# A new start of the written order of a recurrence and a two-layer product: three leading products of zeros fewer, the summing matrices finished in four steps

## The chip, the cores and the metric

One Trainium2 chip, one core. The metric is the device time of one execution in microseconds. The kernel before takes 308.44 us (median of 3 runs, 307.92 to 308.74).

## The reference

First a chunked linear recurrence (4 batches, 8 heads, 768 positions, head width 32, state width 16), then a two-layer product over its 3072 rows of 256:

```python
log_a = np.log(np.clip(a, 1e-06, 1.0))
for c in range(nc):                                  # chunks of 32 positions
    cum = np.cumsum(la, axis=-1)
    L = np.exp(cum[:, :, :, None] - cum[:, :, None, :]) * causal
    M = np.einsum('bhin,bhjn->bhij', Cc, Bc) * L
    y[:, :, sl] = (np.einsum('bhij,bhjd->bhid', M, xc)
                   + np.einsum('bhin,bhnd->bhid', Cc, state) * np.exp(cum)[:, :, :, None])
    Bx = np.einsum('bhjn,bhjd->bhjnd', Bc, xc) * np.exp(cum[:, :, -1:] - cum)[:, :, :, None, None]
    state = np.exp(np.sum(la, axis=-1))[:, :, None, None] * state + np.sum(Bx, axis=2)
...
h = x @ w_in                                         # 256 to 2048
g = np.maximum(h, 0.0) + np.log1p(np.exp(-np.abs(h)))
out = g @ w_out                                      # 2048 to 256
```

## The kernel before

The 768 positions of a batch are six units of 128, 24 units in all, and units go in pairs that share a load tile (`un`). The two products run beside the recurrence as its units become ready; after the recurrence they run alone until the end. Each float32 operand of a large product is split into a rounded part and a rest (`xh`, `xl`, `wih`, `wil`), and three products of the parts are added.

All of it is driven by one written table, `ORDER` (L50), a text of words. The loop at the end of the kernel takes them one by one; a word's name is looked up in `acts` and its numbers are the arguments. `InOrder` and `keep_in_program_order` keep the instructions of every engine, SP's loads too, in the order in which the words emit them. A function that is `staged` does one piece at each of its words, up to its next `yield`. So the table is the order of each engine's queue. `BANKS` holds, digit by digit, which PSUM bank each next request gets.

The words that matter here, with the names that the profile shows:

- `warm3`: products of zeros on TensorE (`some`, 128x512), as many as the number says. They compute nothing that is used.
- `la`, `lr`: loads of the decay factors by column and by row; `loga`, `logr`: a clip on VectorE, then a log on ScalarE; `gb` spreads the log of la (`logs`).
- `kc`: `sums_on_chip` (L201). VectorE fills a tile, GpSimd cuts triangles out of it, and four steps of VectorE make the four summing matrices of 32, 64, 96 and 128 columns.
- `ft`, `fr`: the factors of a batch. Five products of `la` with blocks of `kc` (two passes each), then ScalarE's exponentials `fc` and `ft`; `by_head` on VectorE and a product give `fr`. The growth factors `gg` of the first four units come from `gq` (kc,logs on TensorE).
- `growth`: a scan and an Exp in place of `lr`; `gd`: its store to DRAM in four DMAs; `gg4`: a load from there, the growth factors of the pair 4 and 5. Later pairs have theirs the same way.
- `B` (`bp`), `Q` (C times growth, in place), `C` (`cc`), `A` (`parts_c`, on ScalarE) prepare a pair; `D` makes the masks `rm` on GpSimd; `S` is the score product, `M` weighs it on VectorE (`m`), `U` updates the state, `T` spreads it (`tb`), `R` and `I` make a unit's result, `G` and `X` round it and take the rest (`xh`, `xl`).
- `v`, `un`, `hc`: loads of units. A load tile of `un` can be loaded again when the products that read it are done: the first load behind `w1` goes into the tile of units 4 and 5, whose last reader is `I5`.
- `w4` (and w0, w2, w6): the load of two feature tiles of w_in; `W4`, in pieces, splits it: `ends` on ScalarE, `w` on VectorE, `wih` on ScalarE, `wil` on VectorE. `F`, `H` are the first product over 512 and 256 rows, `P` the parts of its activation (`e`, `gh`, `gl`), `Z` the second product. `F0.4` is the first over 512 rows to read w4's columns. ScalarE loads another activation table ahead of the first `e`.

The three lines that make a staged function:

```python
            if (f, args) not in stages:
                stages[f, args] = f(*args)
            next(stages[f, args], None)
```

Of the kernel before, what the change touches and what calls it, by code (L numbers as in the profile page):

```python
# [999 lines left out]
```

## Time and profile before

| | us |
|---|---|
| median of the runs | 308.44 |
| the profiled execution, its own time | 309.62 |
| its span, first to last instruction | 307.9 |
| TensorE busy (matmuls) | 302.2 |
| VectorE busy | 252.4 |
| ScalarE busy | 176.4 |
| GpSimd busy | 41.1 |

The profiled execution took 309.62 us, of which 307.9 lie between its first and its last instruction. Busy times are sums over the span; they don't tell which engine is waited for at a given moment. Times of the rows further down count from the start of the span.

### The profile page before, as it was taken

The numbers are of one execution on the slowest core, as the hardware profiler recorded it, in microseconds if no ns is written. First come the engines' busy times: TensorE is split into PE (matmuls) and PEld (weight loads), VectorE is DVE, ScalarE is ACT, GpSimd is POOL, SyncE is SP. The second block draws the span as 40 slices with busy tenths as digits, with TensorE's granted clock in tenths as the row PEclk, the third lists the DMA queues.
The fourth block names the chain that finished last, engine by engine and source line by source line (L and its number), as shares of the span: only waits on it lengthen the run. The fifth ranks groups of instructions, "written<-read, shape, count | busy, mean of one in ns | idle before, by whom it ended". The sixth has DMA issues, their size and how long they took to land.

```text
span 307.9 us, 5844 instructions
## 1 busy us (share of the span) xinstructions
PE 302.2 (98%) x2275; PEld 242.9 (79%) x2275; DVE 252.4 (82%) x501; ACT 176.4 (57%) x318; POOL 41.1 (13%) x62
## 2 busy tenths in 40 slices
PE   8999999999999999999999999999999999999995
PEld 5778678778878777788888888888888888888884
DVE  5998898697787868999889898998978858776873
ACT  5568576755755525363666477355566466364662
POOL 2723211440303262100000000000000000000000
PEclk9999999999999999999999999999999999999999
DMA  6992984353203001000010000000012000000003
GB/s 191 311 390 81 351 309 138 131 194 119 73 2 105 0 29 42 2 3 0 33 37 0 0 2 0 0 1 2 1 47 89 2 0 0 1 2 0 0 2 136
DMA packets 10684, 21.77 MB, mean 71 GB/s; under 512 B 1184, under 2 KB 4640, under 8 KB 10656
## 3 DMA queue, kind: packets, MB, share of 16 engines
q1 hardware_dynamic: 10656, 21.40, 20.1%
q8 instruction: 18, 0.29, 0.4%
q14 instruction: 10, 0.08, 0.1%
HBM read 17.85 MB, written 3.54 MB: 69 GB/s over the span
## 4 chain that ended last, share of the span: by engine, by line
PE 91%; DVE 4%; DMA 2%; POOL 1%; issue 1%; ACT 0%; SPq 0%; POOLq 0%
PE sums_at L176 91%; DMA un<-in_un 2%; DVE gl L171 1%; POOL rm L176 1%; DVE wol L171 1%; DVE xl L171 0%; DVE m L171 0%; DVE again L171 0%; DVE state L171 0%; ACT xh L176 0%; SPq L185 0%; DVE cc L171 0%; DVE w L171 0%; DVE bp L171 0%; ACT gh L176 0%
## 5 line engine op out<-in xcount | busy, mean ns | idle before, releaser
L176 PE MATMUL sums_at<-gh,woh 128*128 128x512 f32 (+1 forms) x194 | 76.0, 392 | 0.0
L176 PE MATMUL sums_at<-gl,woh 128*128 128x512 f32 (+1 forms) x194 | 75.4, 389 | 0.0
L176 PE MATMUL sums_at<-gh,wol 128*128 128x512 f32 (+1 forms) x194 | 75.1, 387 | 0.0
L171 DVE TENSOR_TENSOR gl<-e,gh 128x512 fp32r<-128x512 f32 x96 | 63.9, 684 | 12.6 <-ACT gh L176 12.6
L176 ACT CAST gh<-e 128x512 fp32r<-128x512 f32 x96 | 58.7, 620 | 12.5 <-PE sums_at L176 10.8
L176 POOL TENSOR_SCALAR_AFFINE_SELECT rm<-fc 128x512 f32<-128x512 f32 (+1 forms) x52 | 39.8, 789 | 83.8 <-DVE tb L171 19.6
L176 ACT ACTIVATE e<-e 128x512 f32<-128x512 f32 x48 | 30.0, 630 | 23.9 <-DVE e L171 23.8
L176 PEld LDWEIGHTS sums_at<-gh,woh 128*128 128x128 f32 x194 | 36.4, 188 | 8.5 <-issue 0.6
L176 PEld LDWEIGHTS sums_at<-gl,woh 128*128 128x128 f32 x194 | 36.4, 188 | 8.0 <-DVE gl L171 0.8
L176 PEld LDWEIGHTS sums_at<-gh,wol 128*128 128x128 f32 x194 | 36.4, 188 | 7.4
L176 ACT ACTIVATE e<-sums_at 128x512 f32<-128x512 f32 x48 | 28.3, 593 | 23.0 <-PE sums_at L176 18.0
L176 PE MATMUL sums_at<-xh,wih 128*128 128x512 f32 (+1 forms) x104 | 39.8, 383 | 0.0
L176 PE MATMUL sums_at<-xl,wih 128*128 128x512 f32 (+1 forms) x104 | 38.9, 374 | 0.0
L176 PE MATMUL sums_at<-xh,wil 128*128 128x512 f32 (+1 forms) x104 | 38.8, 373 | 0.0
L171 DVE TENSOR_TENSOR e<-sums_at,u 128x512 f32<-128x512 f32 x48 | 32.4, 686 | 6.9 <-PE sums_at L176 6.3
L171 DVE TENSOR_TENSOR m<-sums_at,rm 128x512 f32<-128x512 f32 x48 | 31.4, 685 | 7.3 <-POOL rm L176 4.9
L171 DVE TENSOR_TENSOR u<-sums_at,u 128x512 f32<-128x512 f32 x32 | 22.0, 688 | 4.5 <-PE sums_at L176 3.6
L176 PE MATMUL sums_at<-sxih,sw 128*128 128x512 f32 x64 | 23.8, 390 | 0.0
L176 PEld LDWEIGHTS sums_at<-xh,wih 128*128 128x128 f32 x104 | 19.5, 188 | 4.3
L176 PEld LDWEIGHTS sums_at<-xh,wil 128*128 128x128 f32 x104 | 19.6, 188 | 3.6
L176 PEld LDWEIGHTS sums_at<-xl,wih 128*128 128x128 f32 x104 | 19.6, 188 | 3.2
L176 ACT CAST sw<-sums_w 128x512 fp32r<-128x512 f32 x16 | 9.9, 620 | 13.8 <-DVE sums_w L171 13.7
(109 smaller groups left out, 405.5 us busy)
## 6 DMA issues: line engine op xcount, KB each, us to landing
un<-in_un SPq DMA_DIRECT2D x20, 320.0 KB, 4.6
wraw<-in_w_in SPq DMA_DIRECT2D x8, 511.8 KB, 5.1
wraw<-in_w_out SPq DMA_DIRECT2D x8, 511.8 KB, 6.2
out_t<-o SPq DMA_DIRECT2D x11, 256.0 KB, 2.0
gg<-gd SPq DMA_DIRECT2D x10, 128.0 KB, 5.1
head_in<-in_un SPq DMA_DIRECT2D x4, 192.0 KB, 2.9
head_in<-in_un SPq DMA_DIRECT2D x4, 128.0 KB, 3.1
gd<-lr SPq DMA_DIRECT2D x4, 96.0 KB, 4.5
```

Of the source, the lines that this page charges most:

```text
L171: last_of_v[0] = f(*a, **k)
L176: return lambda *a, **k: tc.keep_in_program_order(f(*a, **k))
```

## The change

The first 195 words of `ORDER` become 199, and the first 45 digits of `BANKS` go with them. The 1080 words from `gg14 X5 F0.5` on are the old ones. As a multiset the new words are the old ones but for two: `warm6` is now `warm3` (so the first real product of TensorE has six products of zeros ahead of it instead of nine), and `kc` stands five times instead of once, since `sums_on_chip` yields ahead of each of its four last steps and is staged now. No other instruction is added or removed; the rest of the change moves instructions within the queues.

```diff
-kc la loga loga gb ends warm1 warm1 warm1 warm6 ft0 lr logr logr growth growth ft0 kb ft0 ft0 fr0 fr2 fr2 D1 fr0
-gq0 gq0 un1 fr0 fr0 un0 hc0 hc1 B0 Q0 C0 hc2 D0 ft0 gq2 warm1 gq2 D0 D0 un3 U0 U1 U0 U1 A0 S0 ft2 ft2 M0 D0 M0
...
-w2 W2 W2 ft2 gd warm1 warm1 T3 G1 X1 S2 w0 W0 un5 W0 M2 W2 M2 fr2 warm1 warm1 fr2 un4 w4 B4 W0 W0 R2 D4 W2 R3 D4
-I3 U3 G3 X3 I2 G2 X2 U4 U3 gg4 Q4 W4 H1 W4 un6 un7 U4 gg6 B6 Q6 D5 A4 D5 w6 W4 H3 T5 F0.1 H0 F0.0 P0.0 S4 F0.3
...
+warm3 la warm1 kc warm1 kc loga kc warm1 un1 loga hc0 lr un0 kb kc ends kc ft0 hc2 hc1 gb logr logr ft0 hc3 ft0
+gq0 growth ft0 gq0 fr0 B0 fr0 gq2 ft0 Q0 fr2 fr0 gq2 D1 fr0 D0 A0 D0 D1 warm1 U0 U1 D1 D0 Q2 U0 fr2 S0 D0 ft2
+fr2 D1 ft2 C2 fr2 un2 un3 growth ft2 M0 C0 M0 ft2 U1 w0 T1 B2 w2 S1 warm1 D3 M1 un4 U2 warm1 A2 ft2 W0 warm1 M1
...
+U3 I2 G3 G2 un7 gd v8 D4 W2 un5 gg4 w4 X2 X3 v10 un6 W2 Q4 A4 W2 v9 w6 gg6 H1 H0 F0.1 D4 D5 P0.1 S4 F0.0 H3 C4
...
         for c in range(NC):
             n = SUB * (c + 1)
+            yield
             V.tensor_scalar(kc[:, c * P : c * P + n], later[:, :n], part[:, c : c + 1], 1.0, op0=ALU.add, op1=ALU.subtract)
...
-        "kc": sums_on_chip,
+        "kc": staged(sums_on_chip),
```

VectorE's queue at the start of the program, before (kc are the summing matrices, la the clip, ends the clearing of two tiles of the weight split):

```order
L171 TENSOR_SCALAR kc_74<-kc_74 128x32
L171 TENSOR_SCALAR kc_74<-kc_74 128x64
L171 TENSOR_SCALAR kc_74<-kc_74 128x96
L171 TENSOR_SCALAR kc_74<-kc_74 128x128
L171 TENSOR_SCALAR la_71<-la_71 128x192
L171 MEMSET ends0_83 128x512
L171 MEMSET ends1_84 128x512
L171 TENSOR_SCALAR lr_72<-lr_72 128x192
```

and in the changed kernel:

```order
L171 TENSOR_SCALAR kc_74<-kc_74 128x32
L171 TENSOR_SCALAR la_71<-la_71 128x192
L171 TENSOR_SCALAR kc_74<-kc_74 128x64
L171 TENSOR_SCALAR kc_74<-kc_74 128x96
L171 MEMSET ends0_83 128x512
L171 MEMSET ends1_84 128x512
L171 TENSOR_SCALAR kc_74<-kc_74 128x128
L171 TENSOR_SCALAR lr_72<-lr_72 128x192
L171 SCALAR_TENSOR_TENSOR cum_73<-keep_82,lr_72 128x192
```

The clip of la comes forward by three places; the fourth step of kc goes behind both clearings.

VectorE's queue further on, before, from the first factors to the first weighing m0 (`head_in<-head_in,gg` is C times growth of the first pair with gg0 and of the second with gg2):

```order
L171 TENSOR_TENSOR by_head2_137<-sums_at_69,kb_75 96x60
L171 TENSOR_TENSOR by_head0_141<-sums_at_69,kb_75 96x60
L171 TENSOR_TENSOR bp0_154<-head_in_80,ft0_130 128x256
L171 TENSOR_TENSOR head_in_80<-head_in_80,gg0_143 128x2x128
L171 TENSOR_TENSOR cc0_157<-head_in_80,fr0_149 128x128
L171 COPY state0_179<-sums_at_69 128x64
L171 SCALAR_TENSOR_TENSOR state1_181<-state0_179,fr0_149,sums_at_69 128x64
L171 TENSOR_TENSOR m0_200<-sums_at_69,rm0_160 128x512 x2
L171 TENSOR_TENSOR tb2_220<-state1_181,kb_75 128x64
```

and in the changed kernel:

```order
L171 TENSOR_TENSOR bp0_142<-head_in_80,ft0_130 128x256
L171 TENSOR_TENSOR by_head0_144<-sums_at_69,kb_75 96x60
L171 TENSOR_TENSOR head_in_80<-head_in_80,gg0_134 128x2x128
L171 TENSOR_TENSOR head_in_80<-head_in_80,gg2_146 128x2x128
L171 COPY state0_175<-sums_at_69 128x64
L171 TENSOR_TENSOR by_head2_177<-sums_at_69,kb_75 96x60
L171 TENSOR_TENSOR cc2_198<-head_in_80,fr0_156 128x256
L171 TENSOR_TENSOR m0_206<-sums_at_69,rm0_158 128x512
L171 TENSOR_TENSOR cc0_208<-head_in_80,fr0_156 128x128
L171 TENSOR_TENSOR m0_206<-sums_at_69,rm0_158 128x512
L171 SCALAR_TENSOR_TENSOR state1_212<-state0_175,fr0_156,sums_at_69 128x64
```

bp0 comes ahead of by_head; the second pair's C times growth and its cc, which stood behind m0 and m1, now stand ahead of m0's two halves or between; the first update of the state (state1) moves behind them.

ScalarE's queue around its second table load, before (ends1_84 with wraw4 is the first piece of w4's split, wih_76 with w4 the third):

```order
L176 CAST ends1_84<-wraw4_323 128x512
L176 ACTIVATE parts_c_85<-un2_310,kb_75 128x256
L176 CAST wih_76<-w4_374 128x2x256
L176 ACT_TABLE_LOAD
L176 ACTIVATE e0_0_426<-sums_at_69 128x512
L176 ACTIVATE e0_1_442<-sums_at_69 128x512
```

and in the changed kernel:

```order
L176 CAST wih_76<-w2_296 128x2x256
L176 ACTIVATE parts_c_85<-un2_235,kb_75 128x256
L176 ACT_TABLE_LOAD
L176 ACTIVATE e0_1_403<-sums_at_69 128x512
L176 CAST ends1_84<-wraw4_367 128x512
L176 CAST wih_76<-w4_431 128x2x256
L176 ACTIVATE e0_0_452<-sums_at_69 128x512
```

Both pieces of w4's split move from ahead of the table load to behind it and behind the first e.

SP's queue from the first load of w_in on, before (gd the stores of lr, gg4 the first load from there):

```order
L185 DMA wraw2_282<-in_w_in 128x2047
L185 DMA gd_81<-lr_72 32x4x192 x4
L185 DMA wraw0_306<-in_w_in 128x2047
L185 DMA un2_310<-in_un 128x640 x2
L185 DMA wraw4_323<-in_w_in 128x2047
L185 DMA gg4_371<-gd_81 128x1x256
```

and in the changed kernel:

```order
L185 DMA wraw0_214<-in_w_in 128x2047
L185 DMA wraw2_220<-in_w_in 128x2047
L185 DMA un2_235<-in_un 128x640
L185 DMA un3_353<-in_un 128x640
L185 DMA gd_81<-lr_72 32x4x192 x4
L185 DMA un4_359<-in_un 128x640
L185 DMA un2_235<-in_un 128x640
L185 DMA gg4_365<-gd_81 128x1x256
L185 DMA wraw4_367<-in_w_in 128x2047
```

The four stores stand behind both w and two units instead of behind one w, and the load of w4 moves from ahead of gg4 to behind it. ScalarE's Exp of lr, which the stores wait for, moves from the fifth place of its queue behind the factors fr2 of the second batch, the fifteenth.

## Rows read from the trace of the kernel before

**Rows 1.** The page's fourth part: shares of the chain that ended last, by engine.
```profile
PE 91%; DVE 4%; DMA 2%; POOL 1%; issue 1%; ACT 0%; SPq 0%; POOLq 0%
```

**Rows 2.** The chain in order of time, whole span: start us, us, what.
```profile
18.27 0.68 issue
18.95 9.38 PE sums_at L176 x131
...
30.15 5.30 DMA un<-in_un
...
35.95 57.49 PE sums_at L176 x597
```

**Rows 3.** Timeline of SP's issues: start us, us, then engine, line, operation, count.
```profile
6.68 2.58 SPq L185 DMA_DIRECT2D gd<-lr  x4
...
12.65 0.58 SPq L185 DMA_DIRECT2D gg<-gd  x1
...
29.10 0.33 SPq L185 DMA_DIRECT2D un<-in_un  x1
```

**Rows 4.** Timeline of TensorE, 25 to 29.2 (columns as before, with partitions, size, type).
```profile
25.39 0.39 PE L176 MATMUL sums_at<-xh,wil 128*128 128x512 f32 x1
...
26.39 0.50 PE L176 MATMUL sums_at<-un 16*128 16x128 f32 x8
...
28.33 0.66 PE L176 MATMUL sums_at<-m,un 128*32 128x128 f32 x16
```

**Rows 5.** Two stretches: us, busy us of each engine, clock, DMA share, GB/s.
```profile
9.85:18.30 8.45, 8.41 (x154) 6.13 (x153) 8.45 (x20) 4.80 (x13) 3.97 (x7) 1.00 0.97 347
23.50:29.00 5.50, 5.50 (x125) 4.44 (x128) 4.47 (x11) 4.01 (x9) 2.48 (x4) 1.00 0.17 64
```

**Rows 6.** Timeline of TensorE, the start; the brackets tell idle time and its releaser.
```profile
0.98 4.02 PE L176 MATMUL sums_at<-some 128*32 128x512 bf16 x9 [0.98 <-POOL some L176]
...
4.93 1.11 PE L176 MATMUL sums_at<-la,kc 128*128 128x96 f32 x4
```

**Rows 7.** Timeline of VectorE, 0 to 23.
```profile
3.68 1.02 DVE L171 MEMSET ends<- 128x512 int32 x2
...
7.01 0.34 DVE L171 TENSOR_TENSOR by_head<-sums_at,kb 96x60 f32<-96x60 f32 x2 [0.81 <-PE sums_at L176]
7.33 0.71 DVE L171 TENSOR_TENSOR bp<-head_in,ft 128x256 f32<-128x256 f32 x1
...
9.85 1.29 DVE L171 TENSOR_TENSOR m<-sums_at,rm 128x512 f32<-128x512 f32 x2 [0.26 <-PE sums_at L176]
...
11.18 0.42 DVE L171 TENSOR_TENSOR bp<-head_in,ft 128x256 f32<-128x256 f32 x1
...
16.91 1.28 DVE L171 TENSOR_TENSOR m<-sums_at,rm 128x512 f32<-128x512 f32 x2
...
20.60 0.52 DVE L171 TENSOR_TENSOR un<-un,gg 128x256 f32<-128x256 f32 x1
...
22.64 0.68 DVE L171 TENSOR_TENSOR wil<-w,wih 128x512 fp32r<-128x512 f32 x1
```

**Rows 8.** Timeline of ScalarE, 6 to 25.
```profile
6.74 0.52 ACT L176 ACTIVATE fc<-sums_at 128x192 f32<-128x192 f32 x1
...
11.03 0.52 ACT L176 ACTIVATE fc<-sums_at 128x192 f32<-128x192 f32 x1 [1.88 <-PE sums_at L176]
...
19.93 0.78 ACT L176 CAST ends<-wraw 128x512 f16<-128x512 bf16 x1
...
22.39 1.28 ACT L176 ACT_TABLE_LOAD   x1
23.68 1.08 ACT L176 ACTIVATE e<-sums_at 128x512 f32<-128x512 f32 x2
```

**Rows 9.** Timeline of GpSimd (POOL), 7 to 24.
```profile
7.33 3.63 POOL L176 TENSOR_SCALAR_AFFINE_SELECT rm<-fc 128x256 f32<-128x256 f32 x8 [4.68 <-ACT ft L176]
```

**Rows 10.** DMA issues from 12.6 to 13.2: KB, us from issue to landing.
```profile
gg<-gd SPq DMA_DIRECT2D x1, 128.0 KB, 6.3
```

More of the change, by code (lines that the diff above doesn't have):

```diff
@@ new lines @@
+fr2 D1 ft2 C2 fr2 un2 un3 growth ft2 M0 C0 M0 ft2 U1 w0 T1 B2 w2 S1 warm1 D3 M1 un4 U2 warm1 A2 ft2 W0 warm1 M1
+U2 T2 T3 warm1 I0 W0 G0 D3 D2 R1 X0 S3 M3 I1 warm1 warm1 W0 W2 G1 M3 warm1 S2 D2 D5 B4 X1 R2 R3 M2 I3 M2 W0 U4
+U3 I2 G3 G2 un7 gd v8 D4 W2 un5 gg4 w4 X2 X3 v10 un6 W2 Q4 A4 W2 v9 w6 gg6 H1 H0 F0.1 D4 D5 P0.1 S4 F0.0 H3 C4
+U3 M4 W4 M4 S5 F0.3 W4 W4 U4 P0.0 P0.1 B10 B6 T5 W4 M5 T4 P0.3 D6 F0.4 P0.4 M5 R4 R5 N10 U7 U6 I4 I5 P0.1 Q6 B8
+U6 U7 N8 A6 G4 G5 D6 H2 gg14 N8 X4 F0.5 X5 P0.4 T7 T10 N10 W6 W6 w1 W1 W1 v13 D7 D7 W6 W6 S6 M6 M6 gg8 Q8 v12
@@ new lines @@
+B12 P0.5 P0.0 w5 F0.2 P0.2 F0.6 C6 w3 S7 M7 M7 N12 I6 R7 I7 w7 W1 W5 W1 Z0.1.1 Z0.1.0 T11 G7 G6 X7 X6 F1.7 W5 W3
+W3 P0.2 F0.7 P0.0 Z0.0.0 W3 P0.3 W3 P0.3 Z0.3.0 gg12 Z0.0.1 Q12 P0.2 Z0.2.1 Z0.3.1 C8 W5 W5 P0.4 Z0.4.0 A8 P0.6
+D9 P0.7 P0.5 N12 W7 D8 D8 W7 W7 W7 w9 T8 P1.7 v16 v17 W9 W9 S8 P0.6 S9 P0.6 A12 F1.4 P1.4 M8 M8 v11 W9 W9 F1.2
+P1.2 Z0.2.0 B16 P0.7 P0.7 Z0.6.0 F1.3 P0.5 Z0.5.0 gg10 w11 Z0.4.1 Q10 C10 D9 T9 Z0.7.1 A10 D11 P1.3 P1.3 D11
+Z0.7.0 E8 M9 M9 w8 J8 K0.0 S10 S11 w14 D10 W8 W8 D10 M10 w10 M10 Z0.5.1 W14 W14 M11 M11 Y8 Y8 C12 v14 v15 P1.2
@@ new lines @@
+D12 P1.2 W8 W8 T13 P1.3 F1.6 W10 D13 D13 P1.4 P1.4 Z0.6.1 K0.1 E10 J10 Y10 w12 W14 S12 S13 M13 P1.6 P1.6 P1.6
+w13 F1.0 P1.0 F0.9 F1.5 D12 P0.9 Z1.3.0 M13 M12 M12 E12 J12 Y12 Y10 N16 B14 N14 Q14 Y12 N14 W12 W12 W11 Z1.3.1
+W14 Z1.2.1 Z1.2.0 gg20 P1.7 P1.0 Z1.6.1 v18 v19 W10 W10 N16 P1.0 Z1.4.0 Z1.6.0 F1.1 P1.1 W10 P1.1 P1.1 Z1.4.1
+D14 D14 W11 W13 B18 Z1.0.0 C14 T14 P1.5 P1.7 A14 F0.11 P0.11 w15 S14 S15 D15 P0.9 P0.9 W12 F0.14 M15 Z1.1.1 T16
+M14 M14 Z1.7.0 W11 Z1.1.0 P0.14 Z1.0.1 P1.5 P1.5 F0.10 P0.10 P0.10 Z1.7.1 Z1.5.1 K1.1 W11 F1.11 P1.11 F0.15
@@ new lines @@
+P0.15 v20 v21 Q20 P0.15 W12 B20 W13 Z0.9.1 gg18 Q18 A18 Z1.5.0 gg16 Q16 A16 C16 T15 E14 N20 T17 D15 M15 J14 Y14
+P0.15 D18 P0.10 K1.0 Y14 xa3.256 v22 N18 W15 N18 T19 N20 T22 F0.8 P0.8 F1.9 W15 W15 S16 S17 B22 D17 D17 M17 M17
+Z0.10.1 F0.13 Z0.10.0 D16 P0.11 Z0.9.0 P0.11 Z0.11.1 Z0.11.0 W13 W13 P1.9 P0.8 P0.8 xa2.0 M16 A20 D16 P0.13
+P0.13 M16 P0.13 W15 F0.12 P0.12 P0.12 P0.12 Z0.8.0 Z0.8.1 E16 N22 N22 J16 Z0.13.1 T23 D18 D19 D19 P0.14 P0.14
+S18 Y16 Y16 S19 C18 E18 Z0.15.0 Z0.15.1 Z0.13.0 gg22 M19 M19 D20 D20 v23 Q22 A22 Z0.12.1 M18 M18 Z0.14.1 L0.1
@@ new lines @@
+J18 D21 D21 C20 S20 S21 M20 M20 Y18 Y18 P1.9 F1.15 P1.15 P1.15 Z0.14.0 Z0.12.0 T21 M21 a1.0.1 k1.0 sw1.0 F1.8
+P1.8 P1.8 P1.9 L0.0 D22 D22 T20 E20 xa2.256 M21 J20 Y20 S22 S23 Y20 M22 Z1.9.0 P1.11 P1.8 F1.10 Z1.8.0 P1.10 D23
+D23 a1.0.2 sw1.0 sw1.0 P1.11 e1.0.0.0 F1.14 Z1.11.0 M23 sw1.0 Z1.11.1 Z1.9.1 M23 C22 E22 M22 J22 P1.14 P1.10
+P1.15 Z1.15.0 P1.10 Z1.10.0 xa3.0 xs1.0 Z1.10.1 xs1.256 xs1.256 Y22 Y22 xa5.256 F1.13 P1.13 F1.12 a1.1.1 Z1.8.1
+Z1.15.1 P1.13 P1.13 Z1.13.1 P1.14 xs1.0 a1.0.7 a1.0.6 a1.0.5 P1.12 P1.12 P1.12 Z1.12.1 Z1.12.0 k1.1 a1.1.2
@@ new lines @@
+e1.0.0.0 e1.0.0.0 Z2.0.0 b1.0 c1.0 e1.0.1.1 P1.14 Z1.14.0 a1.0.3 xa4.0 Z1.13.0 Z1.14.1 sw1.1 e1.1.0.0 e1.1.0.0
+sw1.1 a1.0.4 sw1.1 a1.2.1 k1.2 sw1.1 a1.1.6 e1.0.0.1 a1.1.5 e1.0.0.1 sw1.2 a1.2.2 e1.2.0.0 e1.0.1.0 e1.0.1.0
+a1.1.7 e1.2.0.0 e1.1.0.0 Z2.1.1 Z2.1.0 a1.3.1 b1.1 c1.1 a1.1.4 e1.0.1.0 e1.0.0.1 L1.0 e1.0.1.0 Z2.8.0 e1.0.0.1
+Z3.0.1 k1.3 a1.3.2 Z2.0.1 e1.2.0.0 Z2.2.0 L1.1 Z3.0.0 e1.1.1.1 e1.1.1.0 e1.1.1.0 a1.1.3 e1.3.0.0 a1.4.1 e1.3.0.0
+xa5.0 Z2.8.1 sw1.2 sw1.2 sw1.2 a1.2.6 a1.2.7 e1.1.1.0 e1.1.1.0 Z2.9.0 e1.1.1.1 e1.1.1.1 Z2.2.1 e1.1.0.1 e1.1.0.1
@@ new lines @@
+b1.2 k1.4 a1.2.5 e1.3.0.0 Z2.3.0 Z2.3.1 e1.1.1.1 Z3.9.0 Z3.9.1 a1.4.2 c1.2 a1.2.4 e1.2.1.1 a1.2.3 e1.2.1.1
+e1.2.1.1 e1.1.0.1 sw1.3 sw1.3 sw1.3 Z2.9.1 e1.1.0.1 Z3.1.0 e1.0.1.1 e1.0.1.1 xs2.0 e1.4.0.0 e1.4.0.0 sw1.3
+a1.3.6 a1.5.1 e1.2.1.0 a1.3.7 e1.2.1.0 Z3.1.1 e1.2.0.1 e1.2.1.0 a1.3.5 e1.0.1.1 Z3.8.1 b1.3 Z3.8.0 e1.2.1.1
+Z3.10.0 k1.5 c1.3 e1.3.1.1 a1.3.3 e1.4.0.0 Z2.4.1 Z2.4.0 e1.2.1.0 Z2.10.1 a1.5.2 a1.3.4 e1.2.0.1 e1.2.0.1
+e1.2.0.1 Z2.10.0 T18 sw1.4 sw1.4 sw1.4 e1.3.0.1 e1.3.0.1 Z3.2.0 e1.3.0.1 Z3.2.1 sw1.4 e1.5.0.0 a1.6.1 e1.5.0.0
@@ new lines @@
+a1.4.6 e1.3.1.0 a1.4.5 a1.4.7 Z3.10.1 xa4.256 xs2.256 e1.3.1.1 e1.3.1.1 e1.5.0.0 Z2.5.1 sw1.5 b1.4 k1.6 e1.3.1.0
+e1.3.1.0 c1.4 Z2.5.0 sw1.5 a1.4.4 a1.6.2 e1.4.1.1 a1.4.3 e1.3.1.1 Z3.11.1 e1.4.1.1 e1.4.1.1 e1.3.1.0 Z2.11.0
+sw1.5 e1.4.1.1 Z3.12.0 Z3.12.1 Z2.11.1 sw1.5 a1.5.6 e1.4.0.1 e1.4.0.1 e1.4.1.0 a1.5.5 e1.4.1.0 e1.4.1.0 a1.5.7
+sw1.6 sw1.6 b1.5 e1.3.0.1 Z3.3.0 Z3.3.1 e1.6.0.0 a1.7.1 e1.6.0.0 e1.6.0.0 c1.5 Z3.11.0 a1.5.4 sw1.6 e1.5.1.1
+e1.5.1.1 a1.5.3 sw1.6 e1.5.1.0 a1.6.6 Z2.6.1 a1.6.7 e1.5.1.0 e1.5.1.0 e1.5.0.1 e1.4.1.0 e1.5.0.1 sw1.7 sw1.7
@@ new lines @@
+sw1.7 Z2.12.0 a1.6.5 Z2.6.0 Z2.12.1 b1.6 c1.6 a1.6.4 e1.5.1.0 Z2.13.0 e1.5.1.1 e1.5.1.1 Z3.13.1 sw1.7 a1.7.6
+e1.6.1.0 a1.7.7 k1.7 a1.7.2 e1.6.1.1 a1.6.3 e1.6.1.1 sw2.0 Z3.13.0 b1.7 c1.7 a1.7.4 e1.4.0.1 e1.4.0.1 Z3.4.0
+e1.6.1.0 e1.6.1.0 e1.6.1.0 e1.6.0.1 Z2.14.1 e1.7.1.0 Z2.14.0 a1.7.5 e1.5.0.1 e1.5.0.1 Z3.5.0 Z3.5.1 e1.7.1.1
+a1.7.3 e1.7.1.0 e1.7.1.0 Z2.13.1 sw2.0 sw2.0 e1.7.1.0 Z2.15.1 e1.6.0.1 e1.6.0.1 xs2.256 Z3.4.1 Z2.15.0 sw2.0
+xs2.0 sw2.1 a2.0.7 a2.0.6 e1.7.0.0 a2.0.1 e1.6.1.1 e1.6.1.1 Z3.14.0 e1.7.0.0 e1.7.1.1 e1.7.1.1 e1.7.1.1 Z3.15.1
@@ new lines @@
+k2.0 a2.0.2 e2.0.0.0 sw2.1 sw2.1 e1.6.0.1 Z3.14.1 Z3.6.1 a2.1.1 e1.7.0.0 Z2.7.1 k2.1 L2.1 b2.0 e1.7.0.1 e1.7.0.1
+a2.0.5 Z3.6.0 sw2.2 a2.1.2 c2.0 e2.0.1.1 a2.0.3 e2.0.0.0 e2.0.0.1 e2.0.0.1 Z2.7.0 a2.0.4 sw2.1 a2.1.5 Z3.15.0
+e2.0.1.0 a2.1.6 a2.1.7 e2.0.0.0 Z4.0.0 e1.7.0.1 e1.7.0.1 Z3.7.1 Z3.7.0 e2.0.1.1 e2.0.1.0 sw2.2 e2.0.1.0 L2.0
+e2.0.1.0 Z4.8.1 e2.1.0.0 Z4.8.0 a2.2.1 e2.0.0.1 L3.1 b2.1 sw2.2 c2.1 a2.1.4 e2.1.1.1 L3.0 e2.1.0.0 k2.2 a2.1.3
+e2.0.0.1 a2.2.2 e2.1.0.0 Z5.0.0 Z5.0.1 Z4.1.0 sw2.2 Z4.1.1 a2.2.6 e2.0.1.1 e2.0.1.1 e2.1.0.1 e2.1.1.0 e2.2.0.0
```

52 lines of the change are left out of this document (2 added, 50 removed).

## Prediction

> **What bounds the kernel now.** The page comes first: TensorE holds 91% of the chain that ended last, so its work can't be packed much tighter; only its waits can go [rows 1]. The chain in order of time says where they are [rows 2]. From 35.95 on TensorE runs 57.49 us unbroken, and the words behind the first 199 are the old ones, so what the change wins or loses has to be there by 35.95 us. Going back from there: TensorE waits for VectorE's bp, this for a load of un that takes 5.30 us from its issue at 30.15. SP's rows show why so late [rows 3]: the issue ahead of it but one, another un, goes out at 29.10 only. It writes into the buffer of units 4 and 5, and the last product that reads this is I5: the row that starts at 28.33 takes 0.66 and ends at 28.99 [rows 4], 0.11 ahead of the issue. The DMA engines have little else to do then (share 0.17 from 23.5 to 29) [rows 5], so **the end of I5 carries to the end of the kernel one for one**, and the question is when I5 ends in the changed order. In the order before, TensorE gets to I2 (the product of m2) after 0.68 us of "issue", a wait for nothing that the profile shows, which ends at 18.95 [rows 2]. VectorE has no idle time from 9.85 to 18.3: 8.45 us busy in 8.45 [rows 5].
>
> **The start.** Nine products of zeros take 4.02 us from 0.98, 0.45 each; six end at about 3.6 [rows 6]. The first la,kc pass began at 4.93. It needs the log of la, and la's clip stood behind all four steps of kc; now it follows the first. So the first passes can start more than 1 us earlier. But the fourth step of kc now stands behind both clearings of ends. The same seven instructions as before have ended at 3.68 + 1.02 = 4.70 [rows 7], and the fourth product of the five (pass 7 of 10) reads what that step writes: it can't start before 4.75. Four passes took 1.11 us from 4.93 [rows 6]; the six behind them only about 0.65, until the first factors (fc) at 6.74 [rows 8]: TensorE's pace doubled. Four passes at the slow pace put fc at 4.75 + 1.11 + 0.05 = 5.9: **-0.8 us**. At the fast one it would be near 5.4, -1.3. I take the slow one, because the fast pace began near 5.9 in the order before and no row speaks for an earlier one.
>
> **VectorE up to m2.** bp of the first pair starts at 7.33, after fc and ft, and m2 ends at 16.91 + 1.28 = 18.19: 10.86 us [rows 7]. Ahead of m2 the new order has 0.32 more (both by_head, 7.01 to 7.33, now behind bp), about 0.2 more (a half-size bp of unit 4), 0.60 less (the split of w2, moved behind m2; such instructions come 0.60 apart, two in 1.28), and loses the 0.26 for which m0 waited for TensorE [rows 7]. It also brings the second pair's C times growth and its cc ahead of the end of m0, beside POOL's eight selects, which run for 3.63 us behind the first fc [rows 9]. Beside these bp took 0.71; without them the same shape took 0.42 at 11.18 [rows 7]. So 2 x 0.29 = 0.58 more. The sum is 10.86 + 0.32 + 0.2 - 0.60 - 0.26 + 0.58 = 11.1, from bp's start at 7.33 - 0.8 = 6.53, so m2 ends at 17.6: 0.6 earlier. The collision has 0 and 0.9 as its bounds (none, or each of the two waits a whole select more, 3.63 / 8 = 0.45); 0.58 has a row. The Trainium skill (SBUF — State Buffer, "Who interferes with whom") speaks against the change here: a VectorE instruction with two SBUF inputs contends with a GpSimd instruction that reads SBUF, and the loser blocks fully. By that the forecast would be up to 0.3 later.
>
> **TensorE from I2 to I5.** Without the 0.68 us stall I2 starts 0.1 behind m2, at 17.7 instead of 18.95: -1.25. This isn't kept, because of ScalarE's order. Before, ends(w4) ran at 19.93, ahead of the table load at 22.39, which took 1.28 [rows 8]. Now the whole split of w4 stands behind it. Counted from I2 as before, C times growth of unit 4 starts 1.65 later (20.60 against 18.95) and takes 0.52 [rows 7]; parts_c, as much on ScalarE. That gives 19.35, 19.9 and 20.4; the table load ends at 21.7, one e (1.08 / 2) at 22.2, ends(w4) (0.78) at 23.0. VectorE's split of w4 takes 0.60 to its next start; then state4, bp10, bp6 and tb5, about 0.2 each and 0.3 for the larger, to 24.5, and wil(w4) 0.68: 25.2. In the order before, wil(w4) was done at 22.64 + 0.68 = 23.32, and the first product that reads it is the third of 128x512, at 25.39 [rows 4, 7]: two microseconds to spare, and now none. So that product starts at 25.25. From its start to I5's end were 3.60 us. Of these the S of unit 6 and its parts (eight of the sixteen passes: 0.50; I take 0.65 for all) now come behind I5, and two small updates (0.2) ahead of it [rows 4]: 3.15, and I5 ends at 28.4 instead of 28.99. **Sum: -0.6 us.** With the cover of w4's split gone, each 0.1 us on the chain m2, xh, xl, growth, table load, w4 is 0.1 us of the end.
>
> The price of the table load is the row's: e starts at 23.68, right at the load's end (23.67) [rows 8]. The Trainium skill (ScalarE: Activation LUTs, "What ACT_TABLE_LOAD costs") has 1.28 us for the load, as here, and 1.38 more for a drain. No drain shows in this row; by the page the forecast would be 309.2.
>
> **gd and gg4.** gd, the store of lr, was issued at 6.68, behind lr's Exp [rows 3]. Now that Exp stands behind fr2 and the second batch's fc, which ran at 11.03 [rows 8]; I put its end at 11.3 and gd's first issue at 11.4, 4.7 later. The four issues take 2.58, and everything on SP behind them waits too: two units of un, gg4, w4. The growth of unit 4 must have landed by 19.35. From above: gg4's issue came 5.97 us behind gd's first (12.65), and it landed 6.3 after that, at 18.95 [rows 3, 10]; the same from 11.4 on is 23.7. From below: the DMA engines are full in this stretch (share 0.97, 347 GB/s) [rows 5], so landings follow the bytes issued ahead. Four times 320 KB of un and two w (512 KB) instead of two un and three w are 128 KB more, 0.35 us: 19.3. I take 19.3, since full DMA engines are what the row shows, and the time from issue to landing is then mostly the queue ahead: no cost, and nothing to spare.
>
> The split of kc into steps costs nothing, the instructions are the same; three zeros fewer cost nothing, since TensorE then waits for kc.
>
> **The forecast** in the profile's own time is 309.62 - 0.6 = 309.0; that execution lies 1.18 above the median 308.44, so I predict 307.8. A measurement can tell about 0.3% (0.93 us) from no change, so this counts as the same.
>
> **Rivals.**
> 1. *Faster:* w4's chain is shorter than priced, because the fc passes go at the fast pace (0.5 more) or the collision with POOL is small. Then I5 follows I2, -1.1 to -1.5: about 307.2. For it: the 0.68 us stall alone pays for most. Against: every instruction of the chain has a row. Chance 0.32.
> 2. *Slower:* gg4 is late. Each 0.1 us past 19.35 goes to the end, and from 20.9 on (0.6 + 0.93 past) the kernel is slower by over 0.3%. Issued at about 15.9 (11.4, 2.58 of issues, the last store's landing) with the 6.3 of before, it lands at 22.2: 310.7; a landing 5.0 behind the issue is enough. For it: gd stands 4.7 us later and SP does nothing meanwhile. Against: the bytes ahead of gg4. Chance 0.13.
> 3. *No gain:* the 0.68 us "issue" stall comes back just ahead of I2 (it struck in the updates before I2, and only six instructions fewer stand ahead of that place): 308.5. Or TensorE, with fewer zeros, gets its fast pace later, over all passes of the second batch (ten, 0.1 each, half of it hidden): 308.3. Both are "same". Chance 0.16 together.
> 4. Stall and whole blocks by POOL at once, over +0.93: 0.04.
>
> That leaves 0.35 for the forecast itself: same 0.51, faster 0.32, slower 0.17. The range from 306.9 to 309.4 takes in both bounds of POOL's price and of the pace and leaves out a tenth at either end; the forecast's own is 307.4 to 308.3.
>
> **What would show it.** fc near 5.9; kc's fourth step ending at 4.7; m2 ending near 17.6; no "issue" ahead of I2; ends(w4) behind an e behind the table load; the third 128x512 product waiting for wil(w4); gg4 landing near 19.3; the un after w1 issued near 28.5, and TensorE's restart near 35.4. I am wrong if VectorE waits for gg (slower), if TensorE never waits for wil(w4) (faster), or if the restart isn't tied to I5.

## The result and the profile after

The changed kernel takes 310.88 us (median of 21 executions, 308.83 to 315.54), the kernel before on the same chips 308.63 (21, 307.88 to 309.81). The ratio is 1.0065, with a 95% interval of 1.0048 to 1.0083: slower, where 307.8 and "the same" had been forecast. The ratio leaves out six executions of the changed kernel that lie more than 1.5% above its fastest one; the medians and ranges keep them.

The profiled execution took 311.69 us, with a span of 310.0 (before: 309.62 and 307.9). First the page's shares of the chain that ended last [rows 1]:

```profile
PE 83%; DVE 6%; DMA 5%; ACT 2%; SPq 1%; issue 1%; POOL 1%; ACTq 0%; DVEq 0%; POOLq 0%
```

TensorE's share fell from 91% to 83%: the chain now runs through other engines and DMAs. Where, the chain in order of time says (start, us, what), for the first 45 us [rows 2]:

```profile
13.69 3.97 DMA gd<-lr
17.79 3.59 DMA gg<-gd
...
21.46 0.44 DVE un L171
...
21.97 0.51 ACT parts_c L176
22.50 0.63 ACT L176
...
24.39 0.67 ACT ends L176
25.09 0.69 DVE w L171
...
26.56 0.69 DVE wil L171
...
31.49 6.02 DMA un<-in_un
...
38.01 7.08 PE sums_at L176 x78
```

Read it backwards. TensorE restarts at 38.01 (before 35.95), behind a load of un issued behind I5. (From wil of w4 to SP's issue the chain itself goes through VectorE and ScalarE, 27.25 to 30.87; the wait of SP for TensorE's I5 ends at 30.54, one issue of 0.33 ahead of that, so both ways end together.) I5 is late because of w4's split, this because of the table load and parts_c, these because of C times growth of unit 4 at 21.46. That waits for gg4, and gg4's load waits for the stores gd. SP's issues, the timeline of the same execution [rows 3]:

```profile
11.74 2.56 SPq L185 DMA_DIRECT2D gd<-lr  x4
14.34 1.84 SPq L185 DMA_DIRECT2D un<-in_un  x2
17.79 0.57 SPq L185 DMA_DIRECT2D gg<-gd  x1
18.40 0.59 SPq L185 DMA_DIRECT2D wraw<-in_w_in  x1
...
30.54 0.33 SPq L185 DMA_DIRECT2D un<-in_un  x1
```

gd goes out at 11.74 (before 6.68) and the last of its four stores lands at 13.69 + 3.97 = 17.66. gg4 reads what gd stores, so SP stands until then, and the load goes out at 17.79 (before 12.65) and lands 3.59 later, near 21.4. SP stands twice on this way: 3.6 us for lr's Exp ahead of gd, and 1.5 us for gd's landing ahead of gg4. VectorE's timeline (in brackets idle time and what ended it) [rows 7]:

```profile
5.17 0.26 DVE L171 TENSOR_SCALAR lr<-lr 128x192 f32<-128x192 f32 x1 [0.58 <-DMA lr<-in_al]
...
6.88 0.65 DVE L171 TENSOR_TENSOR bp<-head_in,ft 128x256 f32<-128x256 f32 x1
...
7.74 0.99 DVE L171 TENSOR_TENSOR head_in<-head_in,gg 128x256 f32<-128x256 f32 x2
...
16.58 1.29 DVE L171 TENSOR_TENSOR m<-sums_at,rm 128x512 f32<-128x512 f32 x2 [0.16 <-PE sums_at L176]
...
21.46 0.42 DVE L171 TENSOR_TENSOR un<-un,gg 128x256 f32<-128x256 f32 x1 [1.73 <-DMA gg<-gd]
...
25.09 0.69 DVE L171 SCALAR_TENSOR_TENSOR w<-wraw,ends 128x512 uint32<-128x512 uint32 x1 [0.66 <-ACT ends L176]
...
26.56 0.69 DVE L171 TENSOR_TENSOR wil<-w,wih 128x512 fp32r<-128x512 f32 x1
```

m2 ends at 16.58 + 1.29 = 17.87 (before 18.19): the earlier part did run ahead. Then VectorE waits 1.73 us for gg4. ScalarE [rows 8] and TensorE [rows 4], their timelines:

```profile
5.74 0.51 ACT L176 ACTIVATE fc<-sums_at 128x192 f32<-128x192 f32 x1
...
11.39 0.33 ACT L176 ACTIVATE lr<-lr 128x192 f32<-128x192 f32 x1
...
22.50 1.28 ACT L176 ACT_TABLE_LOAD   x1
23.79 0.60 ACT L176 ACTIVATE e<-sums_at 128x512 f32<-128x512 f32 x1
24.29 0.77 ACT L176 CAST ends<-wraw 128x512 f16<-128x512 bf16 x1
```
```profile
21.94 0.50 PE L176 MATMUL sums_at<-un 16*128 16x128 f32 x8 [1.11 <-DVE un L171]
...
24.44 0.39 PE L176 MATMUL sums_at<-xh,wih 128*128 128x256 f32 x1 [0.50 <-ACT e L176]
...
27.30 0.50 PE L176 MATMUL sums_at<-xh,wil 128*128 128x512 f32 x1
...
29.38 1.06 PE L176 MATMUL sums_at<-m,un 128*32 128x128 f32 x32
```

fc begins 1 us earlier than before (5.74 against 6.74). The second batch's first fc, which lr's Exp now stands behind, begins at 10.97 (before 11.03): the early start does not reach gd. And all of it is lost in the end: the third product of 128x512 starts at 27.30 (before 25.39) and I5's row ends at 30.44 (before 28.99). What SP's standing does to the DMA engines, two stretches of the windows view (us, busy us of five engines, clock, DMA share, GB/s) [rows 5]:

```profile
14.00:18.00 4.00, 4.00 (x107) 3.01 (x107) 3.75 (x9) 1.63 (x4) 2.81 (x4) 1.00 0.77 233
18.00:21.50 3.50, 2.83 (x38) 2.43 (x26) 1.77 (x5) 1.26 (x3) 1.06 (x1) 1.00 0.68 221
```

The DMA engines, at 0.97 in the order before, are not full here: nothing new is issued from 16.18 to 17.79. From the restart to the end the two spans are alike: 307.9 - 35.95 = 271.95 and 310.0 - 38.01 = 271.99.

Medians alone hide a second thing: **the changed kernel's executions spread.** Of the 21, 13 had a mean granted clock of 0.999 or 1.000 and took 308.83 to 311.69 (median 310.44); two with 0.998 took 312.51 and 313.75; six with 0.987 to 0.989 took 313.38 to 315.54. None of the 21 of the kernel before was above 309.81 (of 79 more beside the experiments, two with a clock of 0.994 took 311.31 and 311.76, and all others at most 310.06).

### The profile page after: what moved, and what is told of

It reads as the page before. It is cut to its first block, busy times and chain, and to the rows that moved or that the text cites. A ratio compares the mean times of both kernels' runs of the same rounds, so it can differ in the third digit from the quotient of the medians.

```text
span 310.0 us, 5831 instructions
## 1 busy us (share of the span) xinstructions
PE 301.7 (97%) x2272; PEld 242.9 (78%) x2272; DVE 252.8 (82%) x501; ACT 175.8 (57%) x318; POOL 41.3 (13%) x62
## 4 chain that ended last, share of the span: by engine, by line
PE 83%; DVE 6%; DMA 5%; ACT 2%; SPq 1%; issue 1%; POOL 1%; ACTq 0%; DVEq 0%; POOLq 0%
PE sums_at L176 83%; DMA un<-in_un 2%; DMA gd<-lr 1%; DVE gl L171 1%; SPq L185 1%; DMA gg<-gd 1%; DMA lr<-in_al 1%; DVE m L171 1%; POOL rm L176 1%; DVE bp L171 1%; DVE wol L171 1%; DVE xl L171 0%; DVE w L171 0%; DVE state L171 0%; DVE again L171 0%
## 5 line engine op out<-in xcount | busy, mean ns | idle before, releaser
L171 DVE TENSOR_TENSOR gl<-e,gh 128x512 fp32r<-128x512 f32 x96 | 64.2, 688 | 12.6 <-ACT gh L176 12.6
L176 ACT ACTIVATE e<-sums_at 128x512 f32<-128x512 f32 x48 | 28.4, 594 | 23.0 <-PE sums_at L176 18.0
```

The costliest lines, as they stand in the source:

```text
L171: last_of_v[0] = f(*a, **k)
L176: return lambda *a, **k: tc.keep_in_program_order(f(*a, **k))
```

## The experiments

Two theories were set against each other. **A:** the late Exp of lr, and with it gd and gg4, is what costs. **B:** the cost lies elsewhere (fewer zeros and TensorE's pace, w4's split behind the table load, the start of the program).

**e1_exp_early.** The changed kernel with one word moved: the second `growth`, which emits the Exp of lr, comes ahead of the third `fr0` instead of behind `un3`. SP's order stays.

```diff
-... fr2 fr0 gq2 D1 fr0 D0 A0 ... un2 un3 growth ft2 ...
+... fr2 fr0 gq2 D1 growth fr0 D0 A0 ... un2 un3 ft2 ...
```

> The changed kernel with one word moved: the Exp of lr stands ahead of fr0 on ScalarE instead of behind fr2; SP's order is untouched. Theory (the late growth factors cost the time): gd's first issue at about 8.2 instead of 11.74, gg4 landed well before 19.7, no wait of VectorE for gg (1.73 us now), I5 ends near 28.7, and the kernel takes 308.4 to 309.0, about 2 us less than the changed one. Rival (the split of w4 behind the table load is what costs): gg4 comes in time, but VectorE and TensorE then wait for w4 as long as now and the time stays above 310. Rival (zeros and pace): no change, 310.9.

Measured: 309.54 (12 executions), ratio 1.0042 (1.0016 to 1.0068). SP's timeline:

```profile
8.24 3.08 SPq L185 DMA_DIRECT2D gd<-lr  x4
...
16.16 0.57 SPq L185 DMA_DIRECT2D gg<-gd  x1
...
29.13 0.33 SPq L185 DMA_DIRECT2D un<-in_un  x1
```

gg4 lands 2.5 us after its issue, VectorE has no wait for it, the un behind I5 goes out 1.41 earlier (30.54 to 29.13), and the median falls by 310.88 - 309.54 = 1.34. By the medians A is the larger part, and 0.9 us over the kernel before are left. The difference of the medians is not sharp: the interval of e1's ratio overlaps that of the changed kernel (1.0048 to 1.0083), and among executions at a clock of 0.999 or 1.000 the changed kernel lies 1.8 above the kernel before, e1 0.9. A sharper comparison is that of two kernels further down, e2 (late Exp, nine zeros: 1.0109 to 1.0161) and e13 (early Exp and lr's load second, nine zeros: 1.0015 to 1.0051).

**e7_before_gd_late.** The counter-test in the kernel before: Exp of lr and gd made late, nothing else.

```diff
-... lr logr logr growth growth ft0 ... ft2 ft2 M0 ... W2 ft2 gd warm1 ... U4 U3 gg4 ...
+... lr logr logr growth ft0 ... ft2 ft2 growth M0 ... W2 ft2 warm1 ... U4 U3 gd gg4 ...
```

> The kernel before with the late growth alone: the Exp of lr behind the second batch's fc on ScalarE, the stores gd just ahead of gg4 on SP; all else as before. Theory: gd issued near 11.6, gg4 landing between 20.5 and 21.5, VectorE waits for it and the kernel takes 309.2 to 310.2, 0.6 to 1.6 more than before. Rival (it needs the changed order of the other engines too): 308.6.

Measured: 311.43, ratio 1.0099 (1.007 to 1.0127), more than expected. SP's and VectorE's timelines:

```profile
11.93 2.56 SPq L185 DMA_DIRECT2D gd<-lr  x4
17.87 0.57 SPq L185 DMA_DIRECT2D gg<-gd  x1
```
```profile
21.14 0.43 DVE L171 TENSOR_TENSOR un<-un,gg 128x256 f32<-128x256 f32 x1 [0.49 <-DMA gg<-gd]
...
23.68 0.42 DVE L171 TENSOR_TENSOR bp<-un,ft 128x256 f32<-128x256 f32 x1 [1.32 <-DMA un<-in_un]
...
27.77 0.43 DVE L171 TENSOR_TENSOR bp<-un,ft 128x256 f32<-128x256 f32 x1 [0.71 <-DMA un<-in_un]
```

The wait for gg itself is only 0.49. The rest is the queue: all loads behind gg4 on SP go out late, and VectorE waits 1.32 and 0.71 for two units of un. **A store that SP waits for delays every load behind it**, which theory A had priced too low. So e7 shows that a late gd costs the kernel before 3.1 us, but by another wait than in the changed kernel, where the 1.73 for gg4 itself leads; it doesn't price that wait.

**e4_gd_first.** e1 with gd ahead of the two loads of w.

```diff
-... ft2 U1 w0 T1 B2 w2 S1 ... G2 un7 gd v8 D4 ...
+... ft2 U1 gd w0 T1 B2 w2 S1 ... G2 un7 v8 D4 ...
```

> As e1_exp_early, with the four stores gd also ahead of both loads of w_in on SP, as they were ahead of all but one before. Theory: growth even earlier, but not waited for any more; both w come 2 to 2.5 us later and the first split of w0 (VectorE, 13.49 now, its load landed 12.30) waits, up to 1 us: 308.4 to 309.6, not better than e1. Rival (the growth factors still bind in e1): better than e1 by 0.3 or more.

Measured: 310.31, ratio 1.0059 (1.0045 to 1.0072): no gain over e1. gd now lands 2.0 us after its issue instead of 6.2, gg4 goes out at 13.50, but SP's four issues and its waits make w0 and w2 late (issued at 10.41 against 5.97 in e1), and VectorE's first piece of the split starts at 14.76 instead of 13.90. Moving the store trades one wait for another.

**e2_nine_zeros.** The changed kernel with nine zeros ahead of the first product again.

```diff
-warm3 la warm1 kc ...
+warm6 la warm1 kc ...
```

> The changed kernel with nine leading products of zeros again instead of six. Theory of the late growth factors: the first factors come some 0.5 us later, gd's issue and all behind it by as much at most, so 310.9 to 311.5, no gain. Rival (fewer zeros at the start cost the time, through TensorE's pace): back to about 308.5.

Measured: 312.65, ratio 1.0135 (1.0109 to 1.0161), 1.8 slower than the changed kernel. gd goes out at 12.56 and gg4 at 18.14: the later start makes the late store later. The missing zeros don't cause the loss.

**e3_start_alone.** The kernel before with the new start alone: kc in steps, la's clip behind the first one, six zeros.

```diff
-kc la loga loga gb ends warm1 warm1 warm1 warm6 ft0 ...
+kc la kc loga kc kc kc loga gb ends warm1 warm1 warm1 warm3 ft0 ...
```

> The kernel before with the start alone: kc in steps, la's clip behind the first of them, the other three steps ahead of the clearings, six leading zeros; all else in the old order. Theory: fc comes at about 6.1 instead of 6.74, VectorE is bound from there to m2 and I5 follows, 0.3 to 0.7 us earlier: 307.9 to 308.3. Rival (the 0.68 us stall of TensorE ahead of I2 or a transfer fixes that place): no difference, 308.6.

Measured: 308.94 (12 executions), ratio 1.0014 (0.9992 to 1.0036): no gain. TensorE's timeline:

```profile
3.65 2.45 PE L176 MATMUL sums_at<-la,kc 128*128 128x96 f32 x10
...
8.85 0.61 PE L176 MATMUL sums_at<-some 128*32 128x512 bf16 x1
...
10.64 1.35 PE L176 MATMUL sums_at<-la,kc 128*128 128x96 f32 x10
```

The ten la,kc passes begin at 3.65 instead of 4.93 [rows 6], but take 2.45 instead of 1.78, the zeros at 8.85 take 0.61 where the same row before took 0.39, and the second set starts at 10.64 instead of 9.64. The earlier start is given back by TensorE's pace.

**e5_w4_early.** e1 with three pieces of w4's split ahead of the table load, and w4's load ahead of gg4, so that its data are there.

```diff
-... un5 gg4 w4 X2 X3 v10 un6 W2 Q4 A4 W2 v9 ... D5 P0.1 ... M4 W4 M4 S5 F0.3 W4 W4 U4 ...
+... un5 w4 gg4 X2 X3 v10 un6 W2 W4 Q4 A4 W2 W4 v9 ... D5 W4 P0.1 ... M4 M4 S5 F0.3 U4 ...
```

> As e1_exp_early, with the split of w4 back ahead of ScalarE's table load: ends(w4) ahead of parts_c, wih(w4) ahead of the load, VectorE's split behind wil(w2), and w4's load one place ahead of gg4 on SP. Theory (with gg4 in time, w4's split behind the table load is the second cost): no wait of VectorE for ends(w4), the third 128x512 product 1 us or more earlier, and 308.5 to 309.0, 0.5 to 1.0 us less than e1. Rival (something ahead of m2 sets the end, or the load of w4 comes too late for its new place): no gain over e1, 309.5.

Measured: 312.71, ratio 1.0123 (1.0081 to 1.0166). Worse, but not a clean test: w4's bytes ahead of gg4 delay the growth (VectorE waits 0.72 for gg4), the table load moves from 21.09 in e1 to 22.96, and five of the six executions had a mean clock of 0.995 or less. That the order of w4's split costs something can be neither shown nor excluded with it.

**e6_lr_second.** e1 with the load of lr second instead of fourth, since lr's clip waited 0.58 for it.

```diff
-warm3 la warm1 kc warm1 kc loga kc warm1 un1 loga hc0 lr un0 ...
+warm3 la lr warm1 kc warm1 kc loga kc warm1 un1 loga hc0 un0 ...
```

> As e1_exp_early, with the load of lr in the second place of SP's queue as before instead of the fourth. In e1 lr lands at 5.43 and VectorE's clip, scan and rest of lr stand ahead of the first bp, which starts at 7.29 though its factors are there at 6.3. Theory (the start's gain is eaten by the late load of lr): lr lands near 3.3, bp starts near 6.5, m2 and all behind it 0.5 to 0.8 earlier, 308.7 to 309.0. Rival (the loads of the heads, each one place later, or gg bind): no gain over e1.

Measured: 309.58, ratio 1.0041 (1.0015 to 1.0067), as e1. **e13_early_nine** is e6 with the nine zeros of e2.

```diff
-warm3 la lr warm1 kc ...
+warm6 la lr warm1 kc ...
```

> As e6_lr_second (Exp of lr early, lr loaded second) with nine leading zeros instead of six. Theory (with six zeros TensorE sometimes keeps its slow pace far beyond the first products, which makes the tail of slow executions of the changed kernel): the first product starts at 4.9 instead of 3.65, some of the start is lost, but the passes turn fast before 7 us in its profile and no execution lies above 311; median 309.0 to 309.8. Rival (the tail comes from the loads): executions above 311 as often as in e6 (3 of 12).

Measured: 309.59, ratio 1.0033 (1.0015 to 1.0051). The median stays. One of 12 executions is above 311 (311.15), with two in e1 and three in e6: too few to say that nine zeros make the spread smaller.

**e8_before_look**, the kernel before once more.

> The kernel before unchanged, one more profile. Theory (the profiled execution on which the prediction rests lay 1 us above the median because of its 0.68 us stall ahead of I2): an execution near 308.4 shows no such stall and its I5 ends near 28.0, its restart near 35. Rival (the spread lies elsewhere, in the load behind I5): the stall is there again, or the restart is late by the load's time.

Measured: 308.37, at the median, and without the 0.68 us "issue" wait. The chain from 5 us on:

```profile
5.00 29.70 PE sums_at L176 x450
...
35.48 9.71 PE sums_at L176 x61
```

TensorE runs unbroken to 34.70, and un behind I5 goes out at 28.50 (29.10 in [rows 3]). The load behind that goes out at 29.84 and lands 4.0 us later (5.30 in [rows 2]); TensorE does not wait for it here.

**e12_after_again and e16_after_look**, the changed kernel for its spread.

> The changed kernel unchanged, beside the three others on the same chip: 310.4 to 311.4, and a profile that waits for gg4 on VectorE again by 1 to 2.5 us, if the growth factors are the cause; a profile near 309 without that wait, or one near 311 without it, speaks against it.

> The changed kernel, one more profile. If its time is below 311.7, fast passes before 7 us and a wait of VectorE for gg of 0.5 to 2 us; if it is above 312.5, slow passes until after 9 us and no or a short wait for gg. A time above 312.5 with early fast passes speaks against the second cause.

e12 measured 312.14 (six executions; 310.4 to 311.4 was expected), ratio 1.0113 (1.0063 to 1.0164); its profiled one took 313.81. TensorE's timeline there:

```profile
8.85 0.61 PE L176 MATMUL sums_at<-some 128*32 128x512 bf16 x1
...
11.19 2.45 PE L176 MATMUL sums_at<-la,kc 128*128 128x96 f32 x10
...
16.57 0.63 PE L176 MATMUL sums_at<-some 128*32 128x512 bf16 x1
...
22.14 0.62 PE L176 MATMUL sums_at<-m,head_in 128*32 128x128 f32 x16
```

The second la,kc set takes 2.45 where e3 shows 1.35, and the zeros are slow until 16.57. m2 ends at 22.14 (17.87 in the execution shown above), I2 starts there, and VectorE has no wait for gg4. e16 measured 314.49, and looks different. Three stretches of its windows view (columns as above):

```profile
20.80:22.50 1.70, 0.24 (x3) 0.04 (x1) 0.45 (x2) 0.00 (x0) 0.00 (x0) 1.00 1.00 354
...
23.50:25.00 1.50, 1.50 (x10) 1.36 (x6) 1.48 (x3) 1.49 (x3) 1.26 (x2) 0.50 0.96 385
25.00:26.50 1.50, 1.50 (x7) 1.35 (x6) 0.86 (x3) 0.74 (x2) 0.00 (x0) 0.50 1.01 370
```

The passes are fast from the second set on, VectorE waits 2.07 for gg4, TensorE stands for 1.46 of the first 1.70 us, and then the granted clock is 0.50, the 1.2 GHz level, from 23.5 to 26.5. It falls once more, from 40.6 to 44.0, behind a wait of TensorE of 1.43 for the load behind I5. The Trainium skill (TensorE: Matmul & The Clock Gate, "HAM oscillation — how this bites in real kernels") tells of a kernel that falls to the lower level behind waits for a DMA, and this trace agrees. The wait's length alone doesn't decide it: the execution shown above waited 1.11, and the one of e2 1.67, and both kept 1.00, while e5's fell behind a wait of 1.93. So the expectation that the late fast pace makes the whole spread fell. By their mean clocks, six of the eight longest of the 21 are of e16's kind (0.987 to 0.989; e16 has 0.989). An estimate: 0.011 to 0.013 less clock over 313 us are 3.4 to 4.1 us of TensorE's work, and the median of these six lies 3.9 above that of the 13. The 0.998 of the other two says nothing of e12's kind: e12's own 0.998 comes from its last 1.5 us, behind the last product (clock 0.60), and executions of the kernel before at 308.07 to 309.45 have it too. What made these two long is not known.

**e9_table_early, e10_before_table_early, e11_after_table_early.** e6, the kernel before and the changed kernel with one more activation of 128x1 (Softplus). It computes nothing that is used and writes to a new tile; by it the table is loaded early, behind G1, or in the kernel before (e10, whose edit is shown) behind ends(w4).

```diff
-... U4 U3 gg4 Q4 W4 H1 ...
+... U4 U3 gg4 Q4 W4 tl H1 ...
...
+    stages, early = {}, cp.tile([P, 1], F32, name="early")
...
+        "tl": lambda: A.activation(early, keep[:, 1:2], AF.Softplus),
```

> As e6_lr_second, with ScalarE's second table load moved into its idle time: one 128x1 activation of the kind that needs that table (an extra result that nothing reads) right behind the third-unit xh, near 15.7, so that the load lies between 15.7 and 17.0. Theory (what is left of the loss is the chain growth, parts_c, table load, e, w4 that the new order put in a row): I5 up to 1.2 us earlier than in e6 (28.6), and 308.3 to 308.9, at or below the kernel before. Rival (the rest lies elsewhere): 309.5 as e1 and e6.

> The kernel before with the same extra activation, in ScalarE's idle time ahead of parts_c of unit 4 (near 20.1). Control: in the order before, w4's split is done ahead of the load, TensorE has work until 26 and doesn't wait for e, so no change, 308.4, on the theory; if the table load costs the kernel as such, 307.1 to 307.9.

> The changed kernel with the same extra activation behind the same xh, the Exp of lr and gd left late. Theory: the wait for gg4 stays, the chain behind it gets 1.28 us shorter: 309.7 to 310.2, about 1 us below the changed kernel. Rival: 310.9, if other work (w4, the cover of TensorE) takes the place of the load.

Measured: 315.43 (ratio 1.0191, 1.0141 to 1.0241), 313.14 (1.0136, 1.0102 to 1.017) and 315.87 (1.0222, 1.0173 to 1.0271). All lost, the kernel before too, by 4.6 us. **e14_table_in_place and e15_before_table_in_place** do the same to e6 and to the kernel before, but write over a column of a tile that exists.

```diff
+        "tl": lambda: A.activation(keep[:, 1:2], keep[:, 1:2], AF.Softplus),
```

> As e9_table_early, but the extra activation writes in place into a tile whose values are no longer read, so that no new tile moves the others. If the new tile was what made the products of e9 to e11 slower: 308.3 to 309.2, up to 1.2 us below e6, since the table load leaves the chain from the growth of unit 4 to w4. If the early load as such costs: above 312 again.

> The kernel before with the same extra activation in place, ahead of parts_c of unit 4. If e10's 4.6 us came from the new tile: 308.4, no change, since the load is not waited for in the order before; if from the load: 313 again.

Measured: 310.35 (1.0059, 1.0036 to 1.0081) and 308.3 (0.9988, 0.9973 to 1.0003). In the kernel before an early table load changes nothing, and the 4.6 us were the new tile's. Groups by form, first of e10, then of e15 (busy us, mean ns):

```profile
L176 PE MATMUL sums_at<-gh,woh 128*128 128x512 f32 x190 | 75.9, 400 | 0.0
```
```profile
L176 PE MATMUL sums_at<-gh,woh 128*128 128x512 f32 x190 | 74.9, 394 | 0.0
```

The same product takes 400 ns on average instead of 394, most other large ones 2 to 5 ns more, and TensorE is busy for 306.5 us instead of 302.2. e14 is no gain on e6; in its profiled execution gg4 went out at 17.44 and VectorE waited 1.37 for it again, so it doesn't say what the table load costs in that order. It also shows that the early Exp doesn't always bring gg4 in time: gd's stores landed 6.9 us after their issue there, 5.8 in e6, 6.2 in e1.

## Why the prediction was wrong

**What held.** fc at 5.74 (5.9 forecast; luck, since no pass waited for kc's fourth step: the ten ran without idle time from 3.65, and in e1, e6, e12 and e16 fc began at 6.13 or 6.14), kc's fourth step at 4.59 (4.7), m2's end at 17.87 (17.6), no "issue" wait ahead of I2, ends(w4) behind the first e behind the table load, the third 128x512 product bound by wil(w4), and from there to I5 27.30 to 30.44 = 3.14 (3.15). The table load took its 1.28 and e began 0.01 later: no drain, as in [rows 8]. The collision with POOL was there, and shorter than a whole select (4.14 / 8 = 0.52 in this trace): bp took 0.65 where the same shape took 0.41 at 11.42, and two C times growth took 0.99 together.

**The step that failed** is "the DMA engines are full in this stretch (share 0.97, 347 GB/s) [rows 5], so landings follow the bytes issued ahead", which put gg4's landing at 19.3. It took a share of 0.97 from a stretch in which SP waited for gd only 0.7 us and kept issuing. In the changed order SP itself stands, because gg4 must wait for the landing of gd, and gd had been put at 11.4. gg4's issue was 17.79, its landing 21.37, both later than the bytes say. The slower rival had the mechanism and the point from which it decides (20.9), and put the issue at 15.9; it is the one that came, at a chance of 0.13. It was set low for a reason that holds only while the queue is not waiting. In the profiled execution the sum closes with this step and a longer landing: 309.0 forecast, 27.30 - 25.25 = 2.05 for the third product, and 6.02 - 5.30 = 0.72 for a longer landing of un behind I5, make 311.8; 311.69 was measured. e1 takes the wait away and gets 1.34 of the medians back; e7 puts the late gd into the kernel before and loses 3.1.

**A second step was wrong by itself:** "that execution lies 1.18 above the median, so I predict 307.8". The profiled execution of before contained the 0.68 us "issue" wait; e8, at the median, does not. The -0.6 of the sum took that wait as gained, and the 1.18 took it off once more, in part: of the 1.2 us between the two spans (307.9 and 306.7) 35.95 - 35.48 = 0.47 lie ahead of the restart, the rest behind it. Against e8 the sum of the change without gg4's wait is near nothing: I5 at 28.4 by the forecast, un behind I5 at 28.50 in e8. And "the end of I5 carries to the end of the kernel one for one" held in the two executions compared, but not in e8, where TensorE does not wait for the load behind I5.

**The rest, read from traces alone.** e1, e6 and e13 stay 0.8 to 1.2 us above the kernel before, and un behind I5 goes out at 29.13, 28.67 and 29.19 (e8 28.50, e15 28.41). The third rival's stall did not come back: in e1 VectorE does the two halves of m2 in one row of 1.29 us, as long as ever,

```profile
16.99 1.29 DVE L171 TENSOR_TENSOR m<-sums_at,rm 128x512 f32<-128x512 f32 x2 [0.16 <-PE sums_at L176]
```

and TensorE has no idle time ahead of I2. That rival's other half, a fast pace that comes later, did come in e12, and at a higher price than the 0.5 that it was given. In e6 TensorE loses the lead that it has at I2 partly here, as e1 does:

```profile
22.57 0.38 PE L176 MATMUL sums_at<-xh,wih 128*128 128x256 f32 x1 [0.25 <-ACT e L176]
```

From m2's end to the issue of un are 10.85 us in e1 and e6, as forecast (17.6 to 28.5), and 10.05 in e8 (m2's end 18.45). This names some 0.2 to 0.7 us. The chains of e1, e6 and e13 go here through parts_c, the table load, e and the split of w4, the way that the forecast described. No single edit took it away: not lr's load (e6), not the zeros (e13), not the table load (e14, where gg4 was late again). What of it belongs to w4's place is not shown (e5 was no clean test), and what decides when TensorE's pace turns in an execution stays open. No version tried beats the kernel before; e15 equals it.

**And the spread.** A wait of TensorE can cost more than its length, since the clock can fall behind it (e16). At full clock the changed kernel's median is 310.44, 1.8 above before; the executions with a lower clock make the other 0.4 of its 2.25.

## What to carry to other kernels

Ask of each store whose data are loaded again who waits in the queue between: the price is not the bytes but that the load behind it cannot be issued, nor anything behind that load. A DMA share near 1 says nothing of a stretch in which the issuing queue will itself stand. And before a sum is built on one profiled execution, look whether its stalls are those of the median execution; a stall that the change seems to remove may simply not be there most of the time.

## What the runs showed of the hardware

- **TensorE's pace turns at different times.** Ten la,kc passes take 2.45 us at the slow pace and 1.35 at the fast one (e3's two sets). The clock column says 1.00 for both, but the traces have no clock record ahead of the turn: the first, of 1.00, begins at 4.92 in e13, 10.22 in e3 and 17.26 in e12, where the passes become fast. So the slow pace is taken here for the lower level (1.2 GHz), which no record shows directly. With six zeros ahead the first record begins anywhere from 3.9 (e9) to 17.3 us (e12), with nine between 4.9 and 6.5 in every profile taken.
- **A landing behind I5 varies by a microsecond or more** between executions of the same work: the load of un took 4.0 (e8), 5.3 (before) and 4.7 us (e15), and the load of w_out behind it can be the one that ends last, as in e15's chain:

```profile
30.00 6.80 DMA wraw<-in_w_out
```

- **A new tile of 128x1** slowed most large products of the whole kernel by up to 1.5% (400 against 394 ns for the one shown; TensorE busy 306.5 against 302.2 us), with no instruction of theirs changed (e10 against e15). Why is not shown.
